# The softmax's reciprocals move from VectorE to GpSimd in a top-k attention kernel with an MLP behind it

## The chip, the cores and the metric

The kernel runs on one core of a Trainium2 chip. Such a core has five engines that run beside each other, each with its own queue in order: TensorE (PE in the profile; its weight loads are PEld), VectorE (DVE), ScalarE (ACT), GpSimd (POOL) and SyncE (SP), which here issues the DMAs. The metric is device time in microseconds (us) of one execution. Three runs of the kernel before took 1454.85, 1461.63 and 1463.68 us; the median is 1461.63.

## The reference

The inputs are q, k and v of shape (8, 8, 576, 64) (batch, heads, positions, head size) and two MLP weights, w_in of 512 x 2048 and w_out of 2048 x 512. Every query keeps its 32 largest scores:

```python
scores = scale * np.matmul(q, k.transpose(0, 1, 3, 2))
kth = np.partition(scores, -top_k, axis=-1)[..., -top_k:-top_k + 1]
scores = np.where(scores >= kth, scores, -1000000000.0)
attn = np.exp(scores - np.max(scores, axis=-1, keepdims=True))
attn = attn / (np.sum(attn, axis=-1, keepdims=True) + 1e-09)
x = np.matmul(attn, v)          # then laid out as 4608 tokens x 512
h = x @ w_in
out = np.maximum(0.01 * h, h) @ w_out
```

## The kernel before, in words

The attention is cut into 144 units. A unit is 128 query rows of a pair of heads; the scores of its two heads lie in one tile of 128 x 2 x 576 (`s_sb`, five buffers). The main loop (L648) has one step for each unit and some at the end, and it is a software pipeline whose order is written out by hand: in step s, `cur` is unit s, `old` is unit s-1 and `older` is unit s-2. What a step issues goes to each engine's queue in the order of the code.

- `top_k(cur)` runs on DVE in four slots (L662 to L692). It takes pairwise maxima and minima of the scores (L306), and then four rounds of MAX8 (L311) and match-replace (L314) for each of the two heads, so that the last value of `tops` is the 32nd largest score.
- `mask(old, 0)` and `mask(old, 1)` run on GpSimd. They first compute `nbias` (L322), the negative maximum of both heads; then for each head a penalty `pen` for the scores below the 32nd (L324), which is added to the scores (L325).
- `exponents(old, i)` is ACT's exponential of each head with a running sum (L328); `sums(old)` adds 1e-9 to both sums and writes `ze` (L333), a 128 x 2 tile. Both come late in the step (L681, L695, L696).
- `weights_of(older)` calls `reciprocals`, one 128 x 2 reciprocal on DVE from `ze` to `rz` (L337), and `normalize`, two ACT operations that scale the exponentials by `rz` (L340). It is called at one of three places: at the step's beginning (`at_first`, L661), behind the masks (L668), which is the ordinary case from step 20 on, or behind the second slot (`late`, L676) in most steps before 20.
- `transpose(older)` splits the weights into 16-bit halves on ACT (L349), writes them to DRAM (L350) and fetches them with a transposing DMA (L354). A few units are transposed on PE instead.
- `values` multiplies the transposed weights with v on PE (L393, L405), three steps behind or so; ACT copies the result into `x` (L417).
- `scores` for two coming units is issued on PE at the end of every second step (L235), and ACT copies them from PSUM (L242).
- `mlp_steps(budget)` stands between all these parts, at about seven places of a step. It hands out the MLP's matmuls in small portions: hidden layer (L462, with leaky ReLU on ACT, L468) and output layer (L474, with a copy on ACT, L483). The budget spreads the MLP of a chunk of 256 tokens over the steps until the next chunk's attention is done; the last chunk's MLP is left for the end.

In front of the loop the MLP's weights are loaded and rounded; GpSimd takes part with one copy per piece (L131).

Of the kernel before, what the change touches and what calls it, by code (L numbers as in the profile page):

```python
# [9 lines left out]
F32 = mybir.dt.float32  # L10
# [4 lines left out]
ALU = mybir.AluOpType  # L15
# [5 lines left out]
def kernel(  # L21
# [13 lines left out]
    nc = tc.nc  # L35
    NPAIR, P, S = qT.shape
# [22 lines left out]
    const = ctx.enter_context(tc.tile_pool(name="const", bufs=1))  # L59
# [4 lines left out]
    small = ctx.enter_context(tc.tile_pool(name="small", bufs=5))  # L64
# [8 lines left out]
    nc.vector.tensor_scalar(ident_top, ident, 8.0, None, ALU.mult)  # L73
    ident_low = const.tile([P, P], BF16, name="ident_low")
    nc.vector.tensor_scalar(ident_low, ident, 2.0 ** -23, None, ALU.mult)

    LN2 = math.log(2.0)
    least = const.tile([P, 1], F32, name="least")
# [198 lines left out]
    def keep_scores(u):  # L277

        k = len(kept_of)
        qt, kt = early_of.pop(u)  # L280
        ps = [ps_sc.tile([P, 2, 512], F32, name="wide", bufs=2) if (2 * k + i) % 3 else
              ps_sc.tile([P, 2, 512], F32, name="narrow") for i in range(2)]
        for half in range(2):
            for i, _, side, _ in u.parts:
                d = slice(side * D, (side + 1) * D)
                nc.tensor.matmul(ps[i][:, half, 0:HS], qt[d, :], kt[d, half * HS:(half + 1) * HS],
                                 start=True, stop=True)
        both = gT.rearrange("p f n -> p (f n)")[:, k % 3 * 2 * S:(k % 3 + 1) * 2 * S]
        for i in range(2):
            nc.scalar.copy(both[:, i * S:(i + 1) * S].rearrange("p (h n) -> p h n", h=2), ps[i][:, :, 0:HS])  # L290
        kept_of[u] = kept.tile([P, 2 * S], F32, name=f"kept{k}")
        nc.sync.dma_start(kept_of[u], both)
# [41 lines left out]

    def reciprocals(u):
        u.rz = small.tile([P, 2], F32, name="rz")
        nc.vector.reciprocal(u.rz, u.ze)  # L337

    def normalize(u, i):
        nc.scalar.activation(u.s[i], u.s[i], AF.Copy, bias=0.0, scale=u.rz[:, i:i + 1])  # L340
# [218 lines left out]
    with tc.manual_schedule():  # L559
        last = {p: n for n, u in enumerate(steps) for p in u.pairs}  # L560
        starts = {p: n for n, u in reversed(list(enumerate(steps))) for p in u.pairs}

        to_keep = [[steps[n] for n in (a, a + 1, a + 8, a + 9)] for a in KEPT]
        early_units = {u for us in to_keep for u in us}
        to_load, to_keep = list(to_keep), [u for us in to_keep for u in us]
        assert all(len(u.pairs) == 1 for u in to_keep)

        def score_early(count):

            for _ in range(min(count, len(to_keep))):  # L570
                keep_scores(to_keep.pop(0))
                if len(to_keep) % 4 == 0 and to_load:
                    load_early(to_load.pop(0))

        def load_more(s):

            at_once = 2
            while len(v_of) < NPAIR:
                n = len(v_of)
                due = values_at(starts[n])[0]  # L580
                if n < LOADED_V:
                    load_v(n)
                elif values_at(last[n - LOADED_V])[0] > s:
                    break
                elif due > s + 2:
                    load_v(n, at_once=False)
                elif at_once:
                    load_v(n)
                    at_once -= 1
                else:  # L590
                    break
            while len(qk_of) < NPAIR:
                n = len(qk_of)
                if n < LOADED or not to_keep and n < LOADED + 3:
                    load_qk(n)
                elif not to_keep and last[n - LOADED - 3] + 8 <= s and not waiting:
                    load_qk(n, at_once=False)
                else:
                    break


        for n in range(3):
            load_weights(n)
        jobs = [round_weights(*job) for job in ROUNDED] if AS_WORDS else [iter(())] * len(ROUNDED)
        for n in range(len(jobs) + 1):
            if n == len(jobs) - 1:
                first = first_scores(steps[0])
                next(first, None)
            for job in jobs[max(n - 1, 0):n + 1][::-1]:
                next(job, None)  # L610
            if n == len(jobs) - 1:
                next(first, None)
                load_v(0)
                load_v(1)
            elif n == len(jobs):
                for _ in first_scores(steps[1]):
                    pass
            if n:
                load_weights(n + 2)
            if n >= len(jobs) - 2 and to_load:  # L620
                load_early(to_load.pop(0))
            if 0 <= n - len(jobs) + HP + 1 < HP:
                load_qk(n - len(jobs) + HP + 1)

        def weights_of(u):
            reciprocals(u)
            normalize(u, 0)
            normalize(u, 1)

        def values(*place):  # L630
            due = [u for n, u in enumerate(steps) if values_at(n) == place]
            if not due:
                return ()
            po = ps_sc.tile([P, 2, 512], F32, name="wide", bufs=2)
            if len(due[0].pairs) == 1:
                weigh_whole(due, po, FULL + [NKC - 1] if place[1] == MIDDLE else
                            [QUARTERS] + FULL if place[0] < HURRY else FULL + [QUARTERS])
                return [(due[0], po[:, :, 0:P])]
            for n, u in enumerate(due):
                weigh_left(u, po[:, :, n * LEFT:(n + 1) * LEFT])  # L640
            return [(u, po[:, :, n * LEFT:(n + 1) * LEFT]) for n, u in enumerate(due)]

        def keep(weighed, *place):
            for u, po in weighed:
                keep_values(u.pairs[0], po, u.b, u.q0)
            attended(*place)

        for s in range(len(steps) + LAG + 1):  # L648
            assert s < 7 or not to_keep
            cur, old, older, new = unit(s), unit(s - 1), unit(s - 2), ()  # L650
            if s % 2 == 0:
                new = [u for u in steps[s + 2:s + 4] if u]
            picks = top_k(cur) if cur else iter(())
            budget = slot_budget(s)

            def slot():
                next(picks, None)

            at_first = s < HURRY and s - 2 in HURRIED
            if at_first:  # L660
                weights_of(older)  # L661
            slot()  # L662
            if old:
                mask(old, 0)
                mask(old, 1)
            late = s < HURRY and not {s - 1, s - 2} & set(HURRIED)
            if older and not late and not at_first:
                weights_of(older)  # L668
            mlp_steps(budget)
            weighed = values(s, MIDDLE)  # L670
            at_once = s - 2 in HASTY or any(at == (s, MIDDLE) for at, _ in ready_at)
            if at_once:
                keep(weighed, s, MIDDLE)
            slot()
            if older and late:
                weights_of(older)  # L676
            if s - 2 in HASTY:
                transpose_in_haste(older)
            mlp_steps(budget)
            if old:  # L680
                exponents(old, 0)  # L681
            mlp_steps(budget)
            if older:
                keep_transposed(older) if s - 2 in HASTY else transpose(older, lambda: mlp_steps(budget))
            if not older or s - 2 in HASTY:
                mlp_steps(budget)
            if unit(s + 3) in early_units:
                fetch_scores(unit(s + 3))
            else:
                load_waiting()  # L690
            slot()
            slot()  # L692
            mlp_steps(budget)
            if old:
                exponents(old, 1)  # L695
                sums(old)  # L696
            mlp_steps(budget)
            if not at_once:
                keep(weighed, s, MIDDLE)
            if new and new[0] in early_units:  # L700
                new = ()
            if new and s < HURRY:
                scores(new)
            keep(values(s, END), s, END)
            if new and s >= HURRY:
                scores(new)
            score_early(EARLY_SCORES.get(s, 0))
            budget = slot_budget(s + 1)
            mlp_steps(budget)
            load_more(s)  # L710
        mlp_steps(1e9)
# [59 lines left out]
```

## Time and profile before

One execution was profiled. Its own time is 1456.84 us, its span in the profile 1454.8 us.

| | value |
|---|---|
| median of three runs | 1461.63 us |
| profiled execution | 1456.84 us (span 1454.8 us) |
| TensorE clock granted, mean | 0.987 of full speed |
| start of the first unit's reciprocal | 83.4 us |
| start of the last unit's reciprocal | 1375.5 us |
| GpSimd busy, 260 to 1375 us | 918.5 of 1115 us |
| ACT busy, 260 to 1375 us | 875.2 of 1115 us |
| ACT's waits for DVE's reciprocal | 38.5 us in 43 waits |

How to read the lines further down: a line of a group gives the source line (L337), the engine, the operation, the tile written and the tiles read, shapes, and the number of instructions; behind the bar stand busy time in us and the mean length of one in ns; behind the second bar the idle time of the engine just before these instructions and what ended most of it. A line of the order of time gives start and length in us, then engine, line and operation, and in brackets the idle time ahead of it.

### The profile page before, as it was taken

To read this page: it belongs to the slowest core of one execution; us is meant where nothing else is said; L and a number is where in the kernel's file an instruction comes from. 1 tells how busy PE (TensorE), PEld (TensorE's weight loads), DVE (VectorE), ACT (ScalarE), POOL (GpSimd) and SP (SyncE) were. 2 spreads that over 40 slices of the span, in tenths; PEclk is the share of its full clock that TensorE was granted. 3 is DMA by queue.
4 is the path that set the end of the run, shared out by engine and by line. 5 is a ranking of instruction groups with operands and counts; after the bars stand their busy time and mean duration, and the time that the engine had idled before them with its cause. 6 is when DMAs were issued, how large, how long until landed. Compare 5 with 4: busy or idle time off the path is not lost.

```text
span 1454.8 us, 26041 instructions
## 1 busy us (share of the span) xinstructions
PE 1395.0 (96%) x8980; PEld 902.3 (62%) x8980; DVE 1319.3 (91%) x3401; ACT 1100.8 (76%) x1984; POOL 1096.9 (75%) x744
## 2 busy tenths in 40 slices
PE   7848999999999999999999999999999999999998
PEld 2324548575757576757575767676667666666674
DVE  7999999999999999999999999999999999999500
ACT  8878888777788787777777787878778787778710
POOL 3287888888888888788887788888788888878600
PEclk9968999999999999999999999999999999999999
DMA  8967543666566645666566645666656655544610
GB/s 328 337 222 220 146 121 94 185 159 165 150 181 173 170 138 152 175 185 190 157 166 169 171 138 156 168 192 172 169 162 175 164 152 145 159 138 123 154 40 14
DMA packets 394996, 239.14 MB, mean 164 GB/s; under 512 B 334576, under 2 KB 336112, under 8 KB 392944
## 3 DMA queue, kind: packets, MB, share of 16 engines
q1 hardware_dynamic: 394864, 237.48, 58.3%
q8 instruction: 70, 1.15, 0.3%
q14 instruction: 62, 0.51, 0.1%
HBM read 55.77 MB, written 99.09 MB: 106 GB/s over the span
## 4 chain that ended last, share of the span: by engine, by line
PE 82%; DVE 7%; DMA 5%; ACT 4%; issue 1%; POOL 0%; DVEq 0%; SPq 0%; ACTq 0%; POOLq 0%
PE pz L474 31%; PE ph L462 30%; PE wide L393 10%; PE wide L235 5%; DMA wT<-apart 3%; PE narrow L235 3%; DVE tops L311 2%; DVE pairs L314 2%; PE wide L405 1%; ACT split L349 1%; DMA raw<-in_weights_dram 1%; PE ph L430 1%; DMA apart<-split 1%; ACT s_sb L340 1%; ACT s_sb L328 1%
## 5 line engine op out<-in xcount | busy, mean ns | idle before, releaser
L324 POOL TENSOR_SCALAR pen<-s_sb,tops 128x576 f32<-128x576 f32 x288 | 637.5, 2214 | 196.3 <-DVE tops L311 129.3
L311 DVE MAX8 tops<-pairs 128x8 f32<-128x288 f32 (+1 forms) x1152 | 636.1, 591 | 0.0
L474 PE MATMUL pz<-w_out,gT 128*128 128x512 f32 x1152 | 504.7, 594 | 2.4 <-ACT scale L435 2.4
L462 PE MATMUL ph<-x,w_in 128*128 128x256 f32 x2176 | 482.6, 381 | 0.0
L314 DVE MATCH_REPLACE8 pairs<-tops,pairs 128x288 f32<-128x288 f32 (+1 forms) x864 | 460.3, 538 | 0.0
L462 PEld LDWEIGHTS ph<-x,w_in 128*128 128x128 f32 x2176 | 409.5, 190 | 77.7 <-issue 23.5
L325 POOL TENSOR_TENSOR s_sb<-s_sb,pen 128x576 f32<-128x576 f32 x288 | 406.7, 1412 | 24.1
L474 PEld LDWEIGHTS pz<-w_out,gT 128*128 128x128 f32 x1152 | 216.4, 190 | 266.7 <-issue 261.1
L349 ACT COPY split<-s_sb 128x1152 uint16<-128x1152 uint16 x280 | 309.4, 1146 | 0.1
L340 ACT ACTIVATE s_sb<-s_sb,rz 128x576 f32<-128x576 f32 x288 | 207.6, 773 | 38.6 <-DVE rz L337 38.5
L328 ACT ACTIVATE s_sb<-s_sb,nbias 128x576 f32<-128x576 f32 x288 | 222.3, 772 | 5.7 <-POOL s_sb L325 5.7
L306 DVE TENSOR_TENSOR pairs<-s_sb 128x576 f32<-128x576 f32 x288 | 213.6, 780 | 9.8 <-ACT s_sb L328 0.5
L393 PE MATMUL wide<-wT,vt 128*64 128x128 f32 (+1 forms) x2560 | 158.3, 282 | 15.6 <-DMA wT<-apart 10.8
L393 PEld LDWEIGHTS wide<-wT,vt 128*64 128x64 f32 (+1 forms) x2560 | 130.4, 137 | 64.5 <-issue 39.6
L417 ACT COPY x<-wide 128x128 f32<-128x128 f32 (+1 forms) x160 | 32.2, 260 | 125.1 <-PE wide L393 111.9
L468 ACT ACTIVATE gT<-ph 128x512 f32<-128x512 f32 x136 | 80.6, 592 | 55.1 <-PE ph L462 54.9
L242 ACT COPY s_sb<-wide 128x704 f32<-128x704 f32 x130 | 98.1, 755 | 8.9 <-PE wide L235 2.9
L483 ACT COPY o_sb<-pz 128x512 f32<-128x512 f32 x36 | 21.1, 585 | 92.1 <-PE pz L474 92.1
L235 PE MATMUL wide<-kt,qt 64*64 64x352 f32 x704 | 73.2, 479 | 0.7 <-ACT s_sb L257 0.7
L242 ACT COPY s_sb<-narrow 128x448 f32<-128x448 f32 x130 | 62.9, 536 | 0.6
L314 DVE MATCH_VALUE_LOAD pairs<-tops,pairs 128x8 f32 x864 | 62.8, 73 | 0.0
L328 ACT ACTIVATION_READ_ACCUMULATOR s_sb<-s_sb,nbias 128x1 f32 x288 | 55.3, 192 | 0.0
(69 smaller groups left out, 662.2 us busy)
## 6 DMA issues: line engine op xcount, KB each, us to landing
apart<-split SPq DMA_DIRECT2D x280, 288.0 KB, 2.1
raw<-in_weights_dram SPq DMA_DIRECT2D x15, 1024.0 KB, 7.0
vt<-in_vk_dram SPq DMA_DIRECT2D x32, 320.0 KB, 3.6
out_dram<-o_sb SPq DMA_DIRECT2D x36, 256.0 KB, 3.5
kept<-gT SPq DMA_DIRECT2D x12, 576.0 KB, 3.2
s_sb<-kept SPq DMA_DIRECT2D x12, 576.0 KB, 4.9
qt<-in_qT_dram SPq DMA_DIRECT2D x20, 288.0 KB, 3.5
kt<-in_kT_dram SPq DMA_DIRECT2D x20, 288.0 KB, 3.5
```

The costliest lines, as they stand in the source:

```text
L235: nc.tensor.matmul(to[r0:r0 + LEFT, i, :], qt[d, q0:q0 + LEFT], kt[d, k0:k1], start=True, stop=True)
L306: nc.vector.tensor_tensor(pairs[:, :, n, :], u.both[:, :, 0:HS], u.both[:, :, HS:S], op)
L311: nc.vector.max(out=u.tops[:, i, r, :], in_=rest[i])
L314: nc.vector.match_replace(out=rest[i], in_to_replace=u.tops[:, i, r, :], in_values=rest[i], imm_value=LOWEST)
L324: nc.gpsimd.tensor_scalar(pen, u.s[i], u.tops[:, i, ROUNDS - 1, 7:8], MASKED, ALU.is_lt, ALU.mult)
L325: nc.gpsimd.tensor_tensor(u.s[i], u.s[i], pen, ALU.add)
L328: nc.scalar.activation(u.s[i], u.s[i], AF.Exp, bias=u.nbias[:, i:i + 1], scale=SCALE, accum_out=u.z[:, i:i + 1])
L340: nc.scalar.activation(u.s[i], u.s[i], AF.Copy, bias=0.0, scale=u.rz[:, i:i + 1])
L349: nc.scalar.copy(split, pairs[:, :, h])
L393: nc.tensor.matmul(po[n * D:(n + 1) * D, side, 0:P], v_of[u.pairs[0]][k, at, side, :], u.wT[k, at + side * NKC if at + 1 < NKC else at, :] ...
L462: nc.tensor.matmul(ph[:, i, 0:n], w_in[c][:, f * P:(f + 1) * P], x[c][:, 0:n], start=(c == 0), stop=(c == HP - 1),)
L474: nc.tensor.matmul(pz[0:m, 0:DMODEL], gT[:, f, r0:r0 + m], w_out[f // 4][:, f % 4, :], start=(f == 0), stop=(f == NFC - 1),)
```

## The change

The reciprocal leaves DVE. GpSimd computes it in four operations on 128 x 2 tiles: the sums to the power of minus one, and one Newton step (near * (2 - ze * near)). The call moves out of `weights_of` to the beginning of the step, ahead of the top-k's first slot and of `mask(old, ...)`; on GpSimd's queue the four operations on unit s-2 so stand in front of the mask of unit s-1. A constant tile of -1.0 is set once at the kernel's start. The normalization stays where it was.

```diff
+    minus_one = const.tile([P, 2], F32, name="minus_one")
+    nc.gpsimd.memset(minus_one, -1.0)
...
     def reciprocals(u):
         u.rz = small.tile([P, 2], F32, name="rz")
-        nc.vector.reciprocal(u.rz, u.ze)
+        near = small.tile([P, 2], F32, name="near", bufs=2)
+        rest = small.tile([P, 2], F32, name="rest", bufs=2)
+        nc.gpsimd.tensor_tensor(near, u.ze, minus_one, ALU.pow)
+        nc.gpsimd.tensor_tensor(rest, u.ze, near, ALU.mult)
+        nc.gpsimd.tensor_scalar(rest, rest, -1.0, 2.0, ALU.mult, ALU.add)
+        nc.gpsimd.tensor_tensor(u.rz, near, rest, ALU.mult)
...
         def weights_of(u):
-            reciprocals(u)
             normalize(u, 0)
             normalize(u, 1)
...
             at_first = s < HURRY and s - 2 in HURRIED
+            if older:
+                reciprocals(older)
             if at_first:
                 weights_of(older)
             slot()
```

## The prediction

> **What bounds the kernel now.** I read the page's busy shares first, then its costliest groups, then the waits, then the order of time in one step.
>
> ```profile
> PE 1395.0 (96%) x8980; PEld 902.3 (62%) x8980; DVE 1319.3 (91%) x3401; ACT 1100.8 (76%) x1984; POOL 1096.9 (75%) x744
> ...
> L324 POOL TENSOR_SCALAR pen<-s_sb,tops 128x576 f32<-128x576 f32 x288 | 637.5, 2214 | 196.3 <-DVE tops L311 129.3
> ...
> L325 POOL TENSOR_TENSOR s_sb<-s_sb,pen 128x576 f32<-128x576 f32 x288 | 406.7, 1412 | 24.1
> ```
>
> PE is full, and DVE nearly so. In the stretch 78 to 1375 us PE is busy 1261.6 and DVE 1253.3 of 1297 us (sums of two stages asked for). GpSimd is a quarter idle and waits for DVE's maxima: it is the follower of DVE. That looks like room for four small operations. The same groups for the small operations, from the answer that keeps shapes apart:
>
> ```profile
> L322 POOL TENSOR_SCALAR nbias<-tops 128x2 f32<-128x2 f32 x144 | 33.4, 232 | 20.4 <-DVE tops L311 7.6
> L333 ACT ACTIVATE ze<-z 128x2 f32<-128x2 f32 x144 | 29.3, 204 | 4.6
> L337 DVE RECIPROCAL rz<-ze 128x2 f32<-128x2 f32 x144 | 22.1, 154 | 34.5 <-ACT ze L333 34.2
> ```
>
> The reciprocal costs DVE 22.1 us itself and 34.5 us of waiting for the sums: 56.6 us, the most the change can give back there. What decides is the order in time of one ordinary step:
>
> ```profile
> 613.27 1.42 POOL L325 TENSOR_TENSOR s_sb<-s_sb,pen 128x576 f32<-128x576 f32 x1
> ...
> 614.77 0.23 POOL L322 TENSOR_SCALAR nbias<-tops 128x2 f32<-128x2 f32 x1
> ...
> 616.03 2.22 POOL L324 TENSOR_SCALAR pen<-s_sb,tops 128x576 f32<-128x576 f32 x1 [1.02 <-DVE tops L311]
> ...
> 616.69 0.78 ACT L328 ACTIVATE s_sb<-s_sb,nbias 128x576 f32<-128x576 f32 x1
> ...
> 617.37 0.19 ACT L328 ACTIVATION_READ_ACCUMULATOR s_sb<-s_sb,nbias 128x1 f32 x1
> 617.59 0.20 ACT L333 ACTIVATE ze<-z 128x2 f32<-128x2 f32 x1
> ```
>
> Columns: start, length, engine, line. The addition at 613.27 is the last mask operation of one unit (call it u). GpSimd goes on at 616.03 with the mask of unit u+1. The sums of u exist only at 617.79, since ACT can take the second exponential of u only behind that very addition. Over the kernel, 139 of 143 next masks start before the previous unit's sums are ready, by 1.76 us in the median.
>
> **The change part by part.** *Removed:* 144 DVE reciprocals, worth at most 56.6 us on DVE. PE bounds that: in the 1297 us between first and last sums it idles 1297 - 1261.6 = 35 us, so no more than 35 us could reach the end.
>
> *Added at the start:* one memset on GpSimd, 98 ns by its row for `least` (L79). GpSimd then waits 3.37 us for the first weights, which hides it; without that cover 0.1 us.
>
> *Moved:* the reciprocal of unit u is now GpSimd's first work of step u+2, ahead of the mask of u+1. No DMA goes with it and no SP queue is passed. It is moved past GpSimd's five operations of that mask, and they now queue behind a wait for `ze` of u. Who waits for these: the exponentials of u+1 on ACT, behind those in ACT's order the two splits (L349), so the DMA transpose and PE's values. The second exponential and the sum of u+1 feed the next reciprocal. So a ring closes that was open before: last addition of u, exponential, sum, reciprocal on GpSimd, whole mask of u+1, its last addition. One turn is one step. Its length, from rows of this trace:
>
> - `ze` end to GpSimd's start: 0.19 us. Nothing here shows ACT to GpSimd on a real wait; DVE to GpSimd (the fourth round's maximum to L324) is 0.193 in the median.
> - power of minus one on 128x2: p, below.
> - three more 128x2 operations and nbias: four of 0.23 us by the L322 row, each 0.09 behind the one before (the gap from L325 to L322): 1.28 us.
> - to the mask 0.10; first L324 start to last L325 end 7.52 us (all 144 units between 7.50 and 7.54).
> - to the exponential 0.03 (the least seen); exponential, accumulator read and sum 1.10 us (every unit 1.09 to 1.13).
>
> Sum 0.19 + 1.28 + 0.10 + 7.52 + 0.03 + 1.10 = 10.22 us, plus p. A step now takes 9.07 us ((1375.49 - 78.09)/143, from first to last sum). The ring is longer than the step even with p at zero.
>
> *The power.* No row shows one on GpSimd. Below: an ordinary small operation, 0.23 us (L322). Above: the dearest GpSimd row, 2.2 us (L324), which is 576 columns where this has two; a software power over two columns should not reach it. It cannot be a gain, as it replaces nothing on GpSimd. I take 0.5, near the small row because of the two columns, twice it because a power is more than a multiplication.
>
> *The wait for ACT.* Before, the second exponential starts 2.61 us (mean) behind the addition it waits for, so ACT is late. How much of that stays? Between first and second exponential ACT has 2.57 us of work (two splits, half the time one gT); GpSimd needs 3.80 us from the first addition's end to the second's, and the first exponential takes 1.0 of that: 3.57 against 3.80, so ACT is just in time. Ahead of the first exponential ACT must do score copies, x copies and normalize: 1.82 busy plus 1.45, against 5.4 + p us from sums to the first addition's end. What made it late was PE (ACT waits for PE of 111.9, 92.1 and 54.9 us in the waits list), and PE gets about 1.8 us of slack a step. Bounds 0 and 2.6; I take 0.2, near the busy sums.
>
> So a turn is 10.22 + 0.5 + 0.2 = 10.92 us. 143 turns are 1561.6. Before the first sum 78.1 us stay. Behind the last sum 79.3 stay: that is normalize, transpose, values, and the last chunk alone (27.9 us of ph and 27.6 of pz at the trace's end), which cannot begin earlier; the reciprocal adds 1.4 there and ACT may give 4 back. Span 1719; the profiled run has 1456.84 against a span of 1454.8, so 1721. The median shown is 0.3% above the profiled run: 1724.
>
> *Where the DVE gain goes:* DVE's step is some 0.4 us shorter and then it waits on score buffers that are freed a ring later. Nothing of the 56.6 us arrives.
>
> *The rule against the row.* The Trainium skill, Perfetto Trace Analysis, GPSIMD Engine Instruction, says that reported lengths on this engine are not to be trusted, and to take start-to-start spacing. L322 to the next L324 is 1.26 us start to start in most steps, not 0.23. By the rule, five small operations at 1.26 would make the turn about 15 us and the kernel 2350. I keep the row: L324 starts 0.188 to 0.193 us behind DVE's maximum in the middle eight tenths of units, so the spacing is DVE's pace and no cost of L322; behind L325, where nothing is awaited, the next starts in 0.09. A second rule, GPSIMD Engine Reference, Engine selection, speaks against the change: elementwise work belongs on VectorE, GpSimd being about twice as slow. Twice L337 is 0.31 us, four of them 1.23 with no gaps, where I have 1.55 for the four; by the rule 45 us less, still far slower than before.
>
> **The rivals.** *Dear power* (0.15): p is 1 to 2.2 us, vector code replaced by a loop over elements. Two columns speak against, the lack of any row for it. At 1.6 the turn is 12.0: 1884.
>
> *ACT stays late* (0.06): the 2.6 us of lateness persist because x and score copies wait for PE through the shared PSUM buffers, or because the first exponential slips. The turn is 13.3: 2065. The busy sums speak against.
>
> *DVE relief wins* (0.04, the other side): the reciprocals fit into GpSimd's idle gap of about 1 us ahead of L324, and the step becomes DVE's shorter one: 1457 - 35 = 1422, with PE as the floor. It decides at the point where `ze` plus the four operations end before the next maximum does. That needs sums ready about 1.4 us before today's L324 start; they are 1.76 after it. Even without any wait GpSimd's step would be 7.85 + 1.55 = 9.4, over 9.07. Only spans read wholly wrong could bring it about.
>
> *Cheap ring*, the forecast with p 0.23 to 0.9 and ACT 0 to 0.4 late (0.75): turns of 10.45 to 11.5, so 1654 to 1810.
>
> **How the numbers follow.** 1724 is the likeliest case. The range goes from 1655 to 1850, which takes in the lower half of the dear power (p to 1.4) and leaves out some 0.2. A measurement of this kernel can tell about 1% from no change. Slower by over 1% in all cases but the last: 0.95; within 1%, 0.02; faster, 0.03.
>
> **What would show it.** Right: GpSimd's first recip operation waits for ACT's L333 in nearly every step, about 1.3 us from last addition to it; L324's wait for DVE's maxima (129.3 us) vanishes; PE's busy share falls to some 82%, with PE waiting for wT or ACT; period of the sums near 10.9; exponential 2 close behind the addition. Wrong: a period below 10.2 would mean that a row of the ring overlaps what I add up; above 11.6, look at the power's spacing first, then at ACT's delay.

## The result: 1742.7 us, slower by 19%

The changed kernel takes 1742.69 us in the median of four runs (1740.94 to 1743.34), against 1461.61 us before (four runs too): a ratio of 1.1931, with a 95% interval of 1.1891 to 1.1970. The forecast was 1724 us in a range of 1655 to 1850. The profiled execution took 1742.1 us with a span of 1740.3.

Busy time and the chain that ended last, from the page of the changed kernel (its source lines stand 3 further down than before for the masks and exponentials, 8 further down behind the reciprocals):

```profile
PE 1493.1 (86%) x8980; PEld 939.7 (54%) x8980; DVE 1324.4 (76%) x3257; ACT 1106.6 (64%) x1984; POOL 1354.3 (78%) x1321
...
POOL 69%; ACT 10%; DVE 9%; issue 6%; PE 3%; DMA 2%; POOLq 0%; SPq 0%; DVEq 0%; ACTq 0%
...
L342 POOL TENSOR_TENSOR near<-ze,minus_one 128x2 f32<-128x2 f32 x144 | 105.8, 735 | 175.6 <-ACT ze L336 175.6
```

The chain before ran through PE for 82% of the span; now it runs through GpSimd and ACT for 79%. Yet GpSimd is busy for only 78% of the span, so it is no engine that is simply full. Its largest wait stands in the last line: 144 of 144 powers (the first of the four operations) are preceded by a wait for the sums, 1.22 us each.

The waits of the changed kernel (engine and line that waited, what for, total in us, number, longest):

```profile
ACT s_sb L331 <- POOL s_sb L328: 421.7, 278, 3.0
DVE pairs L309 <- ACT s_sb L245: 293.9, 62, 6.9
...
POOL near L342 <- ACT ze L336: 175.6, 144, 1.8
...
POOL pen L327 <- DVE tops L314: 5.7, 1, 5.7
```

The mask's wait for DVE's maxima, 129.3 us before, is down to one wait of 5.7 at the start. DVE, whose reciprocal was taken away, now waits 293.9 us for scores: ACT copies them out of PSUM (L245), and in its queue these copies stand behind the second exponential (L331), which waits for GpSimd's addition. In 60 of the 62 waits ACT works without a gap from that exponential to the copy. And ACT, which was late before, now waits for GpSimd's additions.

One turn of the ring in the order of time, of the changed kernel, from the mask of one unit to the mask of the next:

```profile
701.20 2.23 POOL L327 TENSOR_SCALAR pen<-s_sb,tops 128x576 f32<-128x576 f32 x1
...
707.32 1.40 POOL L328 TENSOR_TENSOR s_sb<-s_sb,pen 128x576 f32<-128x576 f32 x1
...
708.75 0.77 ACT L331 ACTIVATE s_sb<-s_sb,nbias 128x576 f32<-128x576 f32 x1 [0.83 <-POOL s_sb L328]
709.43 0.19 ACT L331 ACTIVATION_READ_ACCUMULATOR s_sb<-s_sb,nbias 128x1 f32 x1
709.65 0.20 ACT L336 ACTIVATE ze<-z 128x2 f32<-128x2 f32 x1
...
709.93 0.72 POOL L342 TENSOR_TENSOR near<-ze,minus_one 128x2 f32<-128x2 f32 x1 [1.21 <-ACT ze L336]
...
710.73 0.19 POOL L343 TENSOR_TENSOR rest<-ze,near 128x2 f32<-128x2 f32 x1
...
711.01 0.19 POOL L344 TENSOR_SCALAR rest<-rest 128x2 f32<-128x2 f32 x1
...
711.29 0.20 POOL L345 TENSOR_TENSOR rz<-near,rest 128x2 f32<-128x2 f32 x1
711.45 0.25 POOL L325 TENSOR_SCALAR nbias<-tops 128x2 f32<-128x2 f32 x1
711.80 2.23 POOL L327 TENSOR_SCALAR pen<-s_sb,tops 128x576 f32<-128x576 f32 x1
```

Before the change the second exponential (here at 708.75) had the whole next mask to hide behind. Here nothing lies beside it: addition, exponential, sum, four operations, nbias, mask, each begins when the one before has ended. This turn takes 10.60 us; the mean from first to last sum is 11.115 us, against 9.073 before. The difference times 143 turns is 292.0 us. The time ahead of the first sum is 0.7 us shorter, the time behind the last 5.8 us shorter. That leaves 285.5 us, the difference of the two spans.

### The profile page after: what moved, and what is told of

Read it like the earlier page. It is cut to its first block, busy times and chain, and to the rows that moved or that the text cites. A ratio compares the mean times of both kernels' runs of the same rounds, so it can differ in the third digit from the quotient of the medians.

```text
span 1740.3 us, 26515 instructions
## 1 busy us (share of the span) xinstructions
PE 1493.1 (86%) x8980; PEld 939.7 (54%) x8980; DVE 1324.4 (76%) x3257; ACT 1106.6 (64%) x1984; POOL 1354.3 (78%) x1321
## 4 chain that ended last, share of the span: by engine, by line
POOL 69%; ACT 10%; DVE 9%; issue 6%; PE 3%; DMA 2%; POOLq 0%; SPq 0%; DVEq 0%; ACTq 0%
POOL pen L327 34%; POOL s_sb L328 21%; ACT s_sb L331 7%; POOL near L342 5%; DVE tops L314 3%; DVE pairs L317 2%; POOL nbias L325 2%; POOL rz L345 2%; POOL rest L343 2%; ACT ze L336 2%; POOL rest L344 2%; PE ph L470 2%; PE pz L482 2%; DVE pairs L309 1%; DMA s_sb<-kept 1%
## 5 line engine op out<-in xcount | busy, mean ns | idle before, releaser
L327 POOL TENSOR_SCALAR pen<-s_sb,tops 128x576 f32<-128x576 f32 x288 | 662.8, 2301 | 34.2 <-DVE tops L314 5.7
L482 PE MATMUL pz<-w_out,gT 128*128 128x512 f32 x1152 | 525.6, 614 | 4.7 <-ACT scale L443 4.6
L470 PE MATMUL ph<-x,w_in 128*128 128x256 f32 x2176 | 512.3, 396 | 15.7 <-ACT gT L476 15.2
L331 ACT ACTIVATE s_sb<-s_sb,nbias 128x576 f32<-128x576 f32 x288 | 223.3, 775 | 422.0 <-POOL s_sb L328 421.7
L470 PEld LDWEIGHTS ph<-x,w_in 128*128 128x128 f32 x2176 | 425.8, 198 | 110.5 <-issue 28.5
L309 DVE TENSOR_TENSOR pairs<-s_sb 128x576 f32<-128x576 f32 x288 | 230.8, 842 | 306.6 <-ACT s_sb L245 293.9
L328 POOL TENSOR_TENSOR s_sb<-s_sb,pen 128x576 f32<-128x576 f32 x288 | 407.6, 1415 | 24.1
L342 POOL TENSOR_TENSOR near<-ze,minus_one 128x2 f32<-128x2 f32 x144 | 105.8, 735 | 175.6 <-ACT ze L336 175.6
L401 PE MATMUL wide<-wT,vt 128*64 128x128 f32 (+1 forms) x2560 | 180.0, 294 | 60.5 <-DMA wT<-apart 46.3
L401 PEld LDWEIGHTS wide<-wT,vt 128*64 128x64 f32 (+1 forms) x2560 | 144.1, 144 | 117.6 <-DMA wT<-apart 55.6
L245 ACT COPY s_sb<-wide 128x704 f32<-128x704 f32 x130 | 100.6, 774 | 1.4 <-PE wide L238 1.0
L238 PE MATMUL wide<-raw 64*64 64x352 f32 x336 | 38.5, 510 | 55.3 <-ACT x L425 55.3
L245 ACT COPY s_sb<-narrow 128x448 f32<-128x448 f32 x130 | 64.7, 565 | 0.6 <-PE narrow L238 0.5
L238 PEld LDWEIGHTS wide<-kt,qt 64*64 64x64 f32 x704 | 23.5, 144 | 75.0 <-ACT x L425 64.9
```

Source lines behind the costliest of these rows:

```text
L309: nc.vector.tensor_tensor(pairs[:, :, n, :], u.both[:, :, 0:HS], u.both[:, :, HS:S], op)
L327: nc.gpsimd.tensor_scalar(pen, u.s[i], u.tops[:, i, ROUNDS - 1, 7:8], MASKED, ALU.is_lt, ALU.mult)
L328: nc.gpsimd.tensor_tensor(u.s[i], u.s[i], pen, ALU.add)
L331: nc.scalar.activation(u.s[i], u.s[i], AF.Exp, bias=u.nbias[:, i:i + 1], scale=SCALE, accum_out=u.z[:, i:i + 1])
L342: nc.gpsimd.tensor_tensor(near, u.ze, minus_one, ALU.pow)
L401: nc.tensor.matmul(po[n * D:(n + 1) * D, side, 0:P], v_of[u.pairs[0]][k, at, side, :], u.wT[k, at + side * NKC if at + 1 < NKC else at, :] ...
```

## The experiments

The theory is the ring: GpSimd waits for a result that needs GpSimd's own last operation and ACT. The main rival is load: four more operations per step on GpSimd cost what they cost, wherever they stand. A third reading is that the early place in the step is bad for any engine. The first two experiments leave the work as it is and take the wait away. Each time below is a median, of two runs for the kernels that are clearly slower and of 9 to 20 for the others; ratios are against the kernel before, measured beside them on the same chip. The changed kernel was timed in another series; its difference from each experiment agrees within 4 us with the difference of their steps, times 143 turns. A step is the mean time from one unit's sums to the next.

### The wait taken away by older sums

```diff
-    def reciprocals(u):
+    def reciprocals(u, ze):
...
-        nc.gpsimd.tensor_tensor(near, u.ze, minus_one, ALU.pow)
-        nc.gpsimd.tensor_tensor(rest, u.ze, near, ALU.mult)
+        nc.gpsimd.tensor_tensor(near, ze, minus_one, ALU.pow)
+        nc.gpsimd.tensor_tensor(rest, ze, near, ALU.mult)
...
             if older:
-                reciprocals(older)
+                reciprocals(older, (unit(s - 3) or older).ze)
```

> The four operations stay where the change put them, in front of the mask, but take the sums of the unit before (s-3 in place of s-2), which have long been there. Left out: each unit is scaled by its predecessor's sums. Ring theory: the loss is the wait for the sums. Without it GpSimd's own work is left, 0.80 + 0.29 + 0.27 + 0.16 us for the four, 0.34 for nbias, 7.52 for the mask and about 0.1: 9.5 us a step, up to 10.0 with the stretching seen in the trace, so 1515 to 1590 us. Load theory (the loss is that GpSimd has more to do, wherever and whenever): 1742 as with the change.

Measured: 1565.47 us, ratio 1.0759 (1.0728 to 1.0791). The step is 9.872 us. GpSimd's power in this kernel, from its groups:

```profile
L342 POOL TENSOR_TENSOR near<-ze,minus_one 128x2 f32<-128x2 f32 x144 | 176.5, 1226 | 1.2 <-ACT ze L336 1.2
```

The wait is gone (1.2 us where it was 175.6) and 177 us of time with it; instructions, engine and place are unchanged. So load alone is not the cause. The loss does not vanish, though: 1565 is still 7.6% above the kernel before. In what is left, GpSimd goes from operation to operation without a wait, and so does DVE, which is busy for 9.69 us of each step where it was 8.76 before. The power itself got longer, 1226 ns where it was 735. The order of time of this kernel shows what lies beside it:

```profile
708.13 1.41 POOL L328 TENSOR_TENSOR s_sb<-s_sb,pen 128x576 f32<-128x576 f32 x1
708.31 2.51 DVE L309 TENSOR_TENSOR pairs<-s_sb 128x576 f32<-128x576 f32 x2
...
709.48 1.24 POOL L342 TENSOR_TENSOR near<-ze,minus_one 128x2 f32<-128x2 f32 x1
```

DVE's two pairwise operations take 2.51 us together where they take 1.52 undisturbed, and the power beside them 1.24 where it takes 0.72. The two engines seem to hold each other up; the fourth experiment tests that. Of the 0.80 us by which the step is still longer than before, the longer power is some 0.51 (1226 against 719 ns undisturbed), which leaves 0.29 for the load itself. This split is an estimate: older sums without the two-input operations were not run.

### The same work behind half of the mask

```diff
-            if older:
-                reciprocals(older)
...
             if old:
                 mask(old, 0)
+            if older and not at_first:
+                reciprocals(older)
+            if old:
                 mask(old, 1)
```

(In the one step with `at_first` the call stays at the step's beginning.)

> The four operations move behind the first head's mask of the next unit (two operations, 3.8 us further on). Same work, result complete. Ring theory: the sums come 1.2 us behind the addition, so 3.8 us cover the wait and it vanishes; 9.5 to 10.0 us a step, 1515 to 1590 us. Load theory: 1742.

Measured: 1586.86 us, ratio 1.0906 (1.0862 to 1.0951), step 9.999 us. Its group of powers and the first of its waits:

```profile
L342 POOL TENSOR_TENSOR near<-ze,minus_one 128x2 f32<-128x2 f32 x144 | 163.5, 1136 | 3.6 <-ACT ze L336 3.6
```
```profile
ACT s_sb L348 <- POOL rz L345: 378.5, 136, 4.7
```

A kernel that computes everything, with the reciprocals on GpSimd, is 156 us faster than the change only because 3.8 us of mask lie ahead of the wait. It stays 9% slower than before: more work on GpSimd, and here too a longer power (1136 ns), count as the smaller part. ACT now waits 378.5 us for the reciprocals, which its normalization needs, but it is GpSimd that has no wait worth naming in the step.

### VectorE's reciprocal at the new place

```diff
         def weights_of(u):
-            reciprocals(u)
             normalize(u, 0)
...
             at_first = s < HURRY and s - 2 in HURRIED
+            if older:
+                reciprocals(older)
```

> VectorE's reciprocal of the kernel before, called at the new place, the step's beginning, ahead of the first round of maxima. Ring theory: DVE now waits for the sums, but the mask of s-1 is not behind that wait; the loop through DVE takes two steps and is 17.6 us long when ACT is prompt (8.8 a step) and 20.2 when it is 2.6 us late (10.1 a step): 1460 to 1600 us, likeliest 1500. If the place alone makes the loss, whatever the engine: about 1740.

Measured: 1454.25 us, ratio 0.9993 (0.9984 to 1.0002): no difference from the kernel before (the step is 0.03 us longer, the time behind the last sum 4 us shorter). The early place costs nothing on an engine whose queue doesn't feed the sums within the same step. DVE's reciprocals in this kernel:

```profile
L337 DVE RECIPROCAL rz<-ze 128x2 f32<-128x2 f32 x144 | 21.5, 149 | 41.0 <-ACT ze L333 40.8
```

DVE waits 40.8 us where it waited 34.2. I had expected some loss (1460 to 1600, likeliest 1500), and that was a miss. ACT, which gets `rz` earlier, starts the second exponential only 0.47 us behind its addition in the mean, where it was 2.61 us. With ACT so prompt, the expectation's own estimate for the loop through DVE is 8.8 us a step, below the 9.07 of the kernel before. That this is why no loss came is argued, not tested.

### Who stretches GpSimd's operations

In the changed kernel some 0.5 us a step lie beyond the undisturbed turn of 10.60 us, and they come in pieces: single small operations take 0.73 instead of 0.19 us, and L327 3.4 instead of 2.2. In every such case (131 of 131 operations that last more than 100 ns beyond the median of their group) a pairwise maximum or minimum of DVE (L309) runs beside it. These read two inputs from SBUF, the memory in which the tiles lie. The next run puts operations with one input in their place.

```diff
+    lowest8 = const.tile([P, 8], F32, name="lowest8")
+    nc.gpsimd.memset(lowest8, LOWEST)
...
-            nc.vector.tensor_tensor(pairs[:, :, n, :], u.both[:, :, 0:HS], u.both[:, :, HS:S], op)
+            nc.vector.match_replace(out=pairs[:, n, :, :].rearrange("p n h -> p (n h)"), in_to_replace=lowest8,
+                                    in_values=u.s[n], imm_value=LOWEST)
```

> The change, with the pairwise maxima and minima on VectorE (two inputs from SBUF) replaced by match-replace operations over 576 columns with one input, which replace nothing and only copy. Left out: pairs holds plain scores, so the 32nd largest value is not found. About the same length on DVE (0.74 against 0.76 us). If GpSimd's occasional 0.5 to 1.2 us stretches come from DVE's two-input operations, they vanish: 76 us less, 1665 us, step 10.6. If they have another cause: 1742 within 1%.

Measured: 1675.13 us, ratio 1.1513 (1.1480 to 1.1547), step 10.638 us. The small operations of the changed kernel, and then of this one:

```profile
L327 POOL TENSOR_SCALAR pen<-s_sb,tops 128x576 f32<-128x576 f32 x288 | 662.8, 2301 | 34.2 <-DVE tops L314 5.7
...
L325 POOL TENSOR_SCALAR nbias<-tops 128x2 f32<-128x2 f32 x144 | 51.0, 354 | 7.6 <-DVE tops L314 7.6
L345 POOL TENSOR_TENSOR rz<-near,rest 128x2 f32<-128x2 f32 x144 | 46.4, 322 | 12.0
```
```profile
L331 POOL TENSOR_SCALAR pen<-s_sb,tops 128x576 f32<-128x576 f32 x288 | 639.3, 2220 | 34.1 <-ACT gT L296 5.7
...
L329 POOL TENSOR_SCALAR nbias<-tops 128x2 f32<-128x2 f32 x144 | 36.0, 250 | 7.5 <-DVE tops L318 7.5
L349 POOL TENSOR_TENSOR rz<-near,rest 128x2 f32<-128x2 f32 x144 | 28.1, 195 | 12.0
```

With one-input operations of DVE in their place the stretches are gone: mean lengths fall to the undisturbed ones (354 to 250, 322 to 195, 2301 to 2220 ns), although DVE's copies still run beside each kind of GpSimd's small operations in 57 to 63 of 144 cases. So DVE's pairwise operations are the cause of the stretches, 68 us of the loss. That it is their second input fits, but the replacement is also another kind of operation, and the run does not separate the two. The ring stays without them.

### One small operation out of the ring, and three fewer in it

```diff
+    def biases(u):
...
+        nc.gpsimd.tensor_scalar(u.nbias, u.tops[:, :, 0, 0], -SCALE, None, ALU.mult)
...
+            if old:
+                biases(old)
             if older:
                 reciprocals(older)
...
-        if i == 0:
...
-            nc.gpsimd.tensor_scalar(u.nbias, u.tops[:, :, 0, 0], -SCALE, None, ALU.mult)
```

> The change, with nbias of the next unit issued ahead of the four operations instead of behind them. The same instructions on every engine; one small operation moves out of the ring into the time in which GpSimd waits for the sums. Ring theory: 0.17 to 0.35 us a step less (the spacing of nbias to its successor is 0.345 in the median), 25 to 50 us in all: 1693 to 1718. Load theory: 1742 within 0.5%.

Measured: 1704.26 us, ratio 1.1707 (1.1682 to 1.1732). The wait for the sums in this kernel:

```profile
POOL near L343 <- ACT ze L337: 108.8, 144, 2.6
```

Not one instruction fewer, only nbias in front of the wait instead of behind it: the wait falls from 175.6 to 108.8 us, since nbias fills part of it, and the time by 38 us, 0.27 us a step. Load cannot give that.

```diff
-        near = small.tile([P, 2], F32, name="near", bufs=2)
-        rest = small.tile([P, 2], F32, name="rest", bufs=2)
-        nc.gpsimd.tensor_tensor(near, u.ze, minus_one, ALU.pow)
-        nc.gpsimd.tensor_tensor(rest, u.ze, near, ALU.mult)
-        nc.gpsimd.tensor_scalar(rest, rest, -1.0, 2.0, ALU.mult, ALU.add)
-        nc.gpsimd.tensor_tensor(u.rz, near, rest, ALU.mult)
+        nc.gpsimd.tensor_tensor(u.rz, u.ze, minus_one, ALU.pow)
```

> The change without the Newton step: the power alone. Left out: the refinement of the reciprocal. Ring theory: three spacings of 0.287, 0.274 and 0.163 us go, and with them some 20 us of stretches that fell on them: 104 to 125 us less, 1618 to 1640, step near 10.3. If GpSimd's small operations were hidden behind something else: 1742.

Measured: 1628.10 us, ratio 1.1184 (1.1160 to 1.1208), step 10.302: 115 us for the Newton step, 0.81 us a turn, of which 0.72 are the undisturbed spacings. Each small operation in the ring is paid in full.

### What the relief of DVE could bring at most

```diff
-        u.rz = small.tile([P, 2], F32, name="rz")
-        nc.vector.reciprocal(u.rz, u.ze)
+        u.rz = u.ze
```

> The kernel before without any reciprocal: the exponentials are multiplied by the sums themselves. Left out: the division. It bounds what taking the reciprocal off DVE can be worth if its new place cost nothing. Theory: PE bounds; of the 56.6 us on DVE at most 35 arrive: 1422 to 1457, likeliest 1445. If DVE were the bound, the 56.6 us would arrive: 1400.

Measured: 1453.37 us, ratio 0.9984 (0.9971 to 0.9998): 3 us, where I thought some 12 likely. Its waits show where the rest of the 34 us of DVE's waiting went:

```profile
DVE pairs L306 <- ACT s_sb L242: 23.5, 23, 2.3
```

DVE no longer waits for the sums and waits for the next scores instead, which PE makes. Even a reciprocal that costs nothing anywhere gains 0.2%.

A milder form kept the reciprocal on DVE and put it behind the second slot in all steps:

```diff
-            late = s < HURRY and not {s - 1, s - 2} & set(HURRIED)
+            late = s >= HURRY or not {s - 1, s - 2} & set(HURRIED)
```

> The kernel before, with reciprocal and normalization behind the second slot in all steps from 20 on too, so that DVE does not wait for the sums. DVE's 34.5 us of waiting go. Theory: PE is the bound and idles only 35 us in the loop, so at most that, and ACT starts later: 1430 to 1470, likeliest 1450.

Measured: 1457.55 us, ratio 1.0009 (1.0000 to 1.0018). The expectation held for the time and failed in its reason: DVE's wait for the sums did not go.

```profile
DVE rz L337 <- ACT ze L333: 34.5, 32, 5.4
```

The later normalization makes ACT later in turn (second exponential 3.94 us behind its addition, before 2.61), so the sums came later by as much. None of the versions that compute the result beats the kernel before by more than a measurement can tell.

## Why the prediction was right, point by point

**The ring.** Right in its members, and nearly in its length, the latter partly by luck. Forecast beside measured; the medians of the pieces make up a turn that nothing disturbs, the means are what the time is made of:

| piece of a turn | forecast, us | measured median, us | measured mean, us |
|---|---|---|---|
| sums to first operation | 0.19 | 0.08 | 0.08 |
| power, to the next start | 0.59 | 0.80 | 0.81 |
| three operations | 0.96 | 0.72 | 0.93 |
| nbias, to the mask's start | 0.33 | 0.35 | 0.45 |
| mask | 7.52 | 7.52 | 7.70 |
| addition to exponential, ACT's lateness included | 0.23 | 0.03 | 0.04 |
| exponential to sums | 1.10 | 1.10 | 1.10 |
| sum | 10.92 | 10.60 | 11.11 |

For an undisturbed turn the forecast was 0.32 us too long, and it had no term for the disturbances, 0.51 us. The two errors cancel in part, which is why 1724 lies so near. The direction and most of the size do not hang on that: at 10.60 us too the turn is far above 9.07.

**The power.** Taken at 0.5 us, it lasts 0.72 and occupies 0.80 to the next start. The choice near the small row was right; it was undersized by 0.2 us, 30 us in all. *Dear power* falls, as the power takes less than its 1 to 2.2 us.

**ACT's lateness.** I kept 0.2 us; hardly 0.01 stayed. The argument from busy sums was right: *ACT stays late* falls, with the waits of ACT for the additions (421.7 us) as the plain sign.

**Stretches.** Here a term was missing. The medians of the pieces add up to 10.60 us, and the run with one-input copies agrees (10.638); the excess of the means over the medians, in the mask, nbias and the three operations, comes from DVE's pairwise operations, 0.48 us a step by that run. In the trace of before, 285 of 288 of these lay wholly inside an L324, at 0.76 us in the median and L324 at its 2.22, so the row of L324 looked safe to carry over. It was not, because the change shifts the operations against each other. After all cancelling 0.2 us a turn remain, times 143 is 28 us; the 5.8 us saved behind the last sum and 0.7 ahead of the first take some back, which leaves 21 us of span between forecast and result. (The last step of the forecast slipped: 0.3% on 1721 us gives 1726, not 1724.)

**The rule on spacing against the row.** The row was right: small operations on GpSimd follow each other in 0.16 to 0.35 us, not 1.26. The rule of a factor of two against VectorE gave 1.23 us for the four; they take 1.52 undisturbed, near the 1.55 forecast. That nearness is luck: the power was taken 0.21 us too short and the other three 0.24 us too long. By the measurement the four together take ten times VectorE's one reciprocal (0.15 us), not eight, and the power alone nearly five times.

**The DVE gain.** Nothing of it arrives, as forecast; DVE's time went into waiting for scores (293.9 us). The forecast named buffers that come free a ring later; the trace shows ACT's copies of the scores queued behind the second exponential instead. The bound of 35 us was a true bound but a loose one: 3 us is what the free reciprocal brings.

**DVE relief wins** falls: the wait is there in 144 of 144 turns, and even without the wait GpSimd's step is 9.87 us (by the estimate above 9.36 without the longer power), against 9.4 estimated and 9.07 before.

**PE's share** was forecast at 82% and is 86%. PE has the same matmuls and is busy for 98 us more (last section). It had room for that.

## What to carry to other kernels

Before an operation moves to an engine with idle time, follow its input back: if it comes, over whatever other engine, from something that the same engine issues just before in the order of its queue, the idle time is no room, and everything between becomes a ring whose pieces add up. The idle share of GpSimd (25%) said nothing about that; the times at which the input is ready and the next instruction starts did. If such a move is wanted all the same, put independent work between producer and consumer on that queue (half a mask gave back 156 us here), and ask first what the relieved engine would gain if the operation were free.

## What the runs showed of the hardware

DVE's pairwise operations, which read two inputs, and operations on GpSimd hold each other up when one starts during the other: a 128x2 operation took 0.73 instead of 0.19 us, and DVE's operation up to 1.99 instead of 0.75; with one-input operations on DVE both vanished. The Trainium skill, SBUF — State Buffer, "SBUF: two separate sides", describes a port pair that the two share as an exclusive lock for a whole instruction. The order of time with the older sums fits: DVE's first operation starts at 708.31, during L328, and the two together end at 710.82, about 1.3 us after L328's end. The 285 cases before, in which such an operation ran at its usual 0.75 us inside a running L324, do not fit. The traces show that the kind of GpSimd's operation matters: with the older sums, 141 of DVE's pairwise operations start inside a running addition (L328), and each of them is stretched, to 1.84 us in the median; before, 286 start inside a running L324, and only 2 of them last over 0.85 us. In the changed kernel 45 of 49 last that long that start inside L328, and 8 of 52 inside L327. What makes L324 different was not tried.

The clock granted to TensorE was lower where PE had more idle time: 1.00 before and 0.96 after in the loop. Two stretches, of before and then of after (start and end, length, busy us of PE, PEld, DVE, ACT and GpSimd with their instructions, clock, DMA share, GB/s):

```profile
260.00:1375.00 1115.00, 1104.18 (x7375) 734.02 (x7374) 1075.15 (x2806) 875.16 (x1610) 918.46 (x614) 1.00 0.61 163
```
```profile
260.00:1667.00 1407.00, 1228.13 (x7668) 792.26 (x7668) 1100.13 (x2735) 906.75 (x1663) 1173.91 (x1138) 0.96 0.49 132
```

The mean L470 matmul takes 396 ns where it took 381. The longer PE time goes with the waiting and is not its cause: none of the edits that loosen the ring touches PE's work, and the clock comes back with each. With steps of 11.11, 10.84, 10.64, 10.30, 10.00, 9.87 and 9.07 us the mean clock of the profiled run was 0.945, 0.955, 0.960, 0.970, 0.977, 0.982 and 0.987.
